# Two rearrangements in the opening of an adaptive-norm transformer block: part of the modulation's second half summed off TensorE, and the second segment's norm placed ahead of the first attention blocks

## The chip, the core and the metric

The kernel is one launch on one core of a Trainium2 chip. The core's engines run side by side, each with its own queue of instructions: TensorE (PE; its weight loads are PEld), VectorE (DVE), ScalarE (ACT), GpSimd (POOL) and SyncE (SP), which here issues nearly all DMAs. The metric is device time in microseconds (us), the median of three runs.

## What is computed

One block of a transformer on 2048 rows of 512 columns, all in float32. A vector `c` gives six rows of 512 by a matrix product (the modulation); two of them, `sa` and `ca`, shift and scale the first norm.

```python
mod = (_silu(c) @ w_mod).reshape(c.shape[0], 6, 1, -1)
sa, ca, ga, sb, cb, gb = (mod[:, i] for i in range(6))
h = _layernorm(x, axis=-1) * (1 + ca) + sa
x = x + ga * _A_ref(h, A_wq, A_wk, A_wv, A_wo, A_beta)      # attention
h = _layernorm(x, axis=-1) * (1 + cb) + sb
x = x + gb * _B_ref(h, B_w_gate, B_w_up, B_w_down)          # (h Wg * h Wu) Wd
# in _A_ref, for each of N = 4 segments of 512 rows, 32 heads of 16:
logits = einsum("bhqd,bhkd->bhqk", qs, ks) * scale + mask   # causal inside the segment
a_dot = einsum("bhqk,bhkd->bhqd", softmax(logits), vs)
a_mem = (phi(qs) @ M) / (phi(qs) . z + 1e-6)                # memory of earlier segments
o = g * a_mem + (1 - g) * a_dot
M = M + phi(ks)^T @ vs;  z = z + sum(phi(ks))               # phi(t) = t + 1 if t > 0 else exp(t)
```

## The kernel before

The rows go in four segments of 512, each as four tiles of 128 rows; the 32 heads go in four groups `g` of eight. A float32 product is made of three products of split numbers (a rounded high part `H` and the rest `L`); scores are made of three bfloat16 parts of keys and queries, which are written to memory (`kd`, `qd`) and read back stacked (`kst`, `qst`).

**The opening** runs alone, before attention starts. SP issues the loads of `c` (into `s_c`), four tiles of `x` (`xload(0)`), and the first half of two columns of blocks of `w_mod` (`wm0_load(0)`), then key, query and value weights among the second half. PE is kept busy by 20 matmuls of zeros (`NWU`, `warm`). `mod0(j)` makes half `j` of `sa` and `ca` on PE: for each block `k` of 128 rows of `w_mod` and each of four blocks of columns a matmul with `s_c[:, k]`, repeated over 96 columns, into bank `mp0[j]` (tile `m`). `ln(...)`, for segment 0 in its `first` form, makes the norm: statistics by `bn_stats` and `bn_aggr`, one over the root of the variance by a logarithm and an exponential on ACT with one Newton step (tiles `sd`, `y`, `a`, `b`, which the profile calls `asd`, `ay`, `aya`, `ayb`), the normalization of the four tiles in place, PE transposes into `atp`, the modulation on ACT (`ahf`), and the split (`ahH`, `ahL`). Then `a_kq(0, g, "k" or "q")` makes keys and queries of a group (`kps`, `qps`, then `kf`, `qf`), cuts them in three, and makes the features `phi` (`phk`, `phq`); `a_v(0)` makes the values (`vps`, `v`). `gates()` makes `gg` and `omg` from `beta`, copies `omg` into the values' tiles on POOL, and scales the head masks `hmg`. `load_g(nm, w, g)` loads and splits a group's weights (`wrk` into `wkH`, `wkL`); the loads land in tiles that `staged` takes from a list of tags.

**The attention loop** (`for v in range(-2, NQ + 1)`, L1151) goes over 32 units of four heads. `q_half` multiplies queries by keys into two alternating banks, and a DVE instruction reduces each result to its row maximum (`nm`); `k_step` makes the scores again with the maximum in them, ACT takes the exponential (`pt`), POOL masks the diagonal, `av_step` multiplies by the values. Between these steps `fill` takes pieces of the next work from the generator `fill_a`: keys and queries of the next groups, the next segment's norm, the memory.

**What sets the order.** PE's instructions are chained in the order in which the code issues them. `CV` and `CA` chain instructions of DVE and ACT in the same way (`Chain`, L39 in the profile); `vec` and `act` leave the order to a scheduler at build time, until `vec.eng = CV` is set at L1149. POOL's order is the scheduler's. In segment 0, `fill_a` loads segment 1's `x` when it comes to group 2, and weaves the first nine steps of that norm (four tiles of statistics, the root, four normalizations) into the matmuls of groups 2 and 3:

```python
if g >= 2 and s + 1 < NSEG:
    if g == 2:
        xts[s + 1] = xload(s + 1)
        lns = a_ln(s + 1)
        Q = weave(Q, lns, (0, 1, 2, 3))
    else:
        K = weave(K, lns, (1,) if s > 0 else (0, 1, 3))
        Q = weave(Q, lns, (0, 1, 2, 3) if s > 0 else (0, 1))
```

For that norm ACT makes `sd` and `y`, and POOL the five small steps. After the loop the second half of the block follows in its own stage, which the change does not touch.

Of the kernel before, what the change touches and what calls it, by code (L numbers as in the profile page):

```python
# [8 lines left out]
F32 = mybir.dt.float32  # L9
F32R = mybir.dt.float32r  # L10
BF = mybir.dt.bfloat16
AF = mybir.ActivationFunctionType
ALU = mybir.AluOpType
# [4 lines left out]
P = 128  # L18
S, D, H, DH, NSEG, L, F = 2048, 512, 32, 16, 4, 512, 1376
KT = D // P  # L20
# [37 lines left out]
def tile_kernel(ctx, tc, x, wq, wk_, wv, wo, beta, w_gate, w_up, w_down, c, w_mod, out):  # L58
    nc = tc.nc
# [24 lines left out]
    def MM(*a, **k):  # L84
        return pe(nc.tensor.matmul(*a, **k))  # L85
# [4 lines left out]
    CV, CA = Chain(tc, nc.vector), Chain(tc, nc.scalar)  # L90
    vec, act = Switch(nc.vector), Switch(nc.scalar)
# [50 lines left out]
    ones = cst.tile([P, P], F32, name="ones")  # L142
# [29 lines left out]
    def ln(pool, hpool, xt, s, sc, sh, pfx, hb, fast):  # L172
# [10 lines left out]
            if not first:  # L183
                yield 0.0
        sd = pool.tile([P, 4], F32, tag="sd", name=f"{pfx}sd{s}", bufs=2)
        A.activation(sd, mv[:, :, 1], AF.Ln, bias=epst[:, 0:1])
        y = pool.tile([P, 4], F32, tag="y", name=f"{pfx}y{s}", bufs=2)
        A.activation(y, sd, AF.Exp, scale=-0.5)
        a = pool.tile([P, 4], F32, tag="ya", name=f"{pfx}ya{s}", bufs=2)
        b = pool.tile([P, 4], F32, tag="yb", name=f"{pfx}yb{s}", bufs=2)  # L190
        eng = CV if first else nc.gpsimd
        eng.tensor_mul(a, y, y)
        if first:
            CV.scalar_tensor_tensor(b, mv[:, :, 1], EPS, a, op0=ALU.add, op1=ALU.mult)
        else:
            eng.tensor_scalar(b, mv[:, :, 1], 1.0, EPS, op0=ALU.mult, op1=ALU.add)
            eng.tensor_mul(b, b, a)
# [44 lines left out]
    def run(gen):  # L242
        try:
            while True:
                next(gen)
        except StopIteration as e:
            return e.value

    apool, ap = open_pool(name="ap", bufs=1)
    PT = 6  # L250
# [374 lines left out]

    pwpool, pw = open_pool(name="pw", bufs=1, reuse_waits="tile")
    papool, pa = open_pool(name="pa", bufs=2, reuse_waits="tile")
    nc.sync.dma_start(s_c, c)
    wm = w_mod.rearrange("(k p) n -> p k n", p=P)

    def load_mod(i):
# [7 lines left out]
    def xload(s):  # L639
        xt = []  # L640
        for t in range(4):
            a = pa.tile([P, D], F32, tag="x", name=f"x{s}_{t}", bufs=4)
            pin(nc.sync.dma_start(a, x[rows(s, t), :]))
            xt.append(a)
        return xt

    xts = {0: xload(0)}
    NWU = 20
    wu = pa.tile([P, 512], BF, tag="rl", name="wu", bufs=1)
    vec.memset(wu, 0.0)  # L650
    wups = psp.tile([P, 2, 512], F32, tag="lk", name="wups", bufs=1)
# [64 lines left out]
        CV.tensor_copy(sa_c[:, 2 * j:2 * j + 2], ps[:, 0:2])  # L716
        CV.tensor_scalar_add(ca_c[:, 2 * j:2 * j + 2], ps[:, 2:4], 1.0)

    def mod0(j):
        ps = mp0[j].rearrange("p (i n) -> p i n", n=P)[:, :, 0:MW]  # L720
        for k in range(KT):
            for i in range(4):
                MM(ps[:, i], r0[j][k][:, i * P:(i + 1) * P], s_c[:, k:k + 1].to_broadcast([P, MW]),
                   start=k == i == 0, stop=k == KT - 1, skip_group_check=True)

    hcur = [None]

    def a_ln(s):
        return ln(pa, pa, xts.pop(s), s, ca_c, sa_c, "a", ("h", 8, 2), s == 0)

    def weave(a, b, at):

        i = 0
        for w in a:
            yield w
            if w:
                for _ in range(at.count(i)):
                    w = next(b, None)
                    if w or w is False:
                        yield w  # L740
                i += 1

    wH, wL = {}, {}
    stage = [("ph", 3), ("ph", 3), ("ph", 3), ("mem", 1), ("pkr", 1), ("f", 2)] + [("x", 4)] * 4 + [("mem", 1), ("memb", 2)]
    nst = [0]

    def staged(nm):
        tg, n = stage[nst[0] % len(stage)]
        nst[0] += 1
        return (ap if tg == "memb" else pa).tile([P, D], F32, tag=tg, name=f"wr{nm}", bufs=n)  # L750

    def load_g(nm, w, g):
# [46 lines left out]
    def a_kq(s, g, nm):  # L799
# [3 lines left out]
        if True:  # L803
# [2 lines left out]
            n = 0  # L806
            three = ((wH, hH), (wH, hL), (wL, hH)) if s == 0 and g < 2 else ((wH, hH), (wL, hH), (wH, hL))
            terms = [(k, *ab) for k in range(KT) for ab in three]
            if s == 0 and g == 1:
                terms.sort(key=lambda t: t[1] is wL)  # L810
            for k, a, b in terms:
                MM(ps, a[nm, g][:, k, :], b[k], start=n == 0, stop=n == 11)
                n += 1
# [2 lines left out]
            f = pa.tile([P, L], F32, tag="f", name=f"{nm}f{s}_{g}", bufs=2)  # L816
            fast = s == 0 and g == 0
            A, V = (CA, CV) if fast else (act, nc.gpsimd)
            A.activation(f, ps, AF.Copy)
            q3 = pa.tile([P, 3, L], BF, tag="q3", name=f"{nm}3_{s}_{g}", bufs=2)  # L820
            r = pa.tile([P, L], F32, tag="qr", name=f"{nm}r_{s}_{g}", bufs=2)
            i0, i1, i2 = (0, 1, 2) if nm == "k" else (2, 1, 0)
# [153 lines left out]
    def fill_a():  # L976
# [1 line left out]
            next(w)  # L978
        yield from av
        memq.extend((a_mem(0, 0), a_mem(0, 1)))  # L980
        lns = None
        for s in range(NSEG):
            if s > 0:
                hcur[0] = yield from lns
# [2 lines left out]
            for g in range(2 if s == 0 else 0, NG):  # L987
# [5 lines left out]
                K, Q = a_kq(s, g, "k"), a_kq(s, g, "q")  # L993
                if s == NSEG - 1 and g == 0:
                    B["orl"] = wo_load(0, wpool)
                if g >= 2 and s + 1 < NSEG:
                    if g == 2:
                        xts[s + 1] = xload(s + 1)
                        lns = a_ln(s + 1)
                        Q = weave(Q, lns, (0, 1, 2, 3))  # L1000
                    else:
                        K = weave(K, lns, (1,) if s > 0 else (0, 1, 3))
                        Q = weave(Q, lns, (0, 1, 2, 3) if s > 0 else (0, 1))
                if g == 1 and 0 < s < 3:
                    acc = mod_acc(r)
                    K, Q = weave(K, acc, (0, 2)), weave(Q, acc, (0, 2))
# [98 lines left out]
    lng = ln(pa, pa, xts.pop(0), 0, ca_c, sa_c, "a", ("h", 8, 2), True)  # L1105
    next(lng)
    mod0(0)
    next(lng)
    mod0_out(0, mp0[0])
    mod0(1)  # L1110
    next(lw[0])
    next(lng)
    next(lng)
# [13 lines left out]
    w1 = [load_g(nm, w, 1) for nm, w in (("k", wk_), ("q", wq))]  # L1127
    for w in w1:
        next(w)
    run(kq0[1])  # L1130
    run(kq0[0])
    load(0)
# [4 lines left out]
        next(w)  # L1137
    for i in range(3):
        next(av)
    gates()  # L1140
    w2 = [load_g(nm, w, 2) for nm, w in (("k", wk_), ("q", wq))]
    for w in w2:
# [536 lines left out]
```

## Time and profile before

| | |
|---|---|
| runs | 854.02, 854.42, 854.63 us; median 854.42 us |
| profiled execution | 853.83 us, of which the span of the trace is 852.1 us |
| busy in the span | PE 98%, DVE 75%, ACT 58%, POOL 32% |
| chain that ended last | PE 60%, DVE 4%, ACT 2%, POOL 2% of the span |
| DMA | 139.57 MB, mean 164 GB/s |
| granted TensorE clock | 1.0 |

Times in the profile count from the span's start. A row of the timeline gives start, duration, engine, line of the kernel, operation, written and read tiles (buffer numbers left out), and in brackets the idle time before it with what ended it. A group's row gives the sum, the mean of one in ns, and the idle time before. A matmul's end is modelled, so two matmuls in a row seem to overlap. Spans on POOL are rough.

### The profile page before, as it was taken

What the parts mean: (1) busy time and instruction counts of PE and PEld (TensorE: products, weight loads), DVE (VectorE), ACT (ScalarE), POOL (GpSimd) and SP (SyncE); (2) the same over time, 40 slices, a digit from 0 to 9 for tenths busy, and PEclk for the clock granted to TensorE, in tenths of its full rate; (3) what the DMA queues carried; (4) which work ended last, traced back from release to release, by engine and by line L of the source; (5) the groups of instructions that cost most, each with busy time, mean ns of one, the idle gap of its engine ahead of it and who ended that gap; (6) DMA issues with size and microseconds to landing.
All of it is one profiled execution on the core that took longest, in us unless ns stands there. A gap on an engine that the chain in (4) does not pass through costs nothing.

```text
span 852.1 us, 14420 instructions
## 1 busy us (share of the span) xinstructions
PE 835.4 (98%) x4982; PEld 598.2 (70%) x4982; DVE 641.9 (75%) x1796; ACT 498.0 (58%) x759; POOL 275.7 (32%) x423
## 2 busy tenths in 40 slices
PE   9989999999999999999999999999999999999998
PEld 6756656666665656656665687887888778888886
DVE  7897868887778967787888359989987855447654
ACT  4758767787676876677545626344435546455230
POOL 2756627566565774675424610000000000000000
PEclk9999999999999999999999999999999999999999
DMA  9655445564545554457675457587650675335102
GB/s 272 153 150 158 111 114 136 164 171 120 144 103 166 146 163 106 123 155 230 173 233 161 137 193 238 187 286 273 233 220 28 234 269 211 123 135 185 42 9 98
DMA packets 83928, 139.57 MB, mean 164 GB/s; under 512 B 12720, under 2 KB 46768, under 8 KB 83856
## 3 DMA queue, kind: packets, MB, share of 16 engines
q1 hardware_dynamic: 83568, 138.52, 52.6%
q8 instruction: 39, 0.64, 0.3%
q14 instruction: 33, 0.27, 0.1%
q10 hardware_dynamic: 288, 0.15, 0.1%
HBM read 89.87 MB, written 48.50 MB: 162 GB/s over the span
## 4 chain that ended last, share of the span: by engine, by line
PE 60%; DVE 4%; ACT 2%; POOL 2%; issue 1%; DMA 0%; DVEq 0%; POOLq 0%; ACTq 0%
PE acc L1355 14%; PE Xu L1286 7%; PE Xg L1286 7%; PE wops L85 5%; PE tb L85 4%; PE Yu L1286 4%; PE Yg L1286 4%; PE k L85 3%; PE q L85 3%; DVE q L39 2%; PE Zg L1286 1%; PE Zu L1286 1%; PE qps L85 1%; PE vps L85 1%; PE ctp L88 1%; PE Xx L1286 1%
## 5 line engine op out<-in xcount | busy, mean ns | idle before, releaser
L39 DVE CUSTOM_DVE_ANT_0 q<-q,cmask 128x384 f32<-128x384 f32 (+3 forms) x512 | 248.3, 503 | 72.2 <-PE q L85 64.6
L335 ACT ACTIVATE pt<-k 128x1024 f32<-128x1024 f32 x160 | 163.9, 1024 | 74.2 <-PE k L85 72.2
L341 POOL TENSOR_SCALAR_AFFINE_SELECT pt<-pt 128x256 f32<-128x256 f32 (+1 forms) x224 | 97.6, 449 | 137.9 <-ACT pt L335 135.9
L85 PE MATMUL q<-kst,qst 96*128 96x384 bf16 (+3 forms) x512 | 122.8, 302 | 6.4 <-DVE nm L39 5.1
L85 PE MATMUL k<-qst,kst 98*128 98x384 bf16 (+3 forms) x512 | 96.0, 299 | 1.6 <-ACT pt L335 1.3
L1363 DVE TENSOR_TENSOR xa<-xa,acc 128x512 f32<-128x512 f32 x95 | 64.9, 684 | 39.1 <-PE acc L1355 38.5
L85 PEld LDWEIGHTS <-qst 96*128 96x128 bf16 x512 | 43.9, 98 | 57.8 <-issue 43.0
L85 PE MATMUL tb<-pt,v 128*32 128x512 f32 (+3 forms) x1024 | 75.7, 436 | 0.3 <-POOL pt L341 0.3
L39 DVE DVE_READ_ACCUMULATOR2_ANT nm<- 128x1 f32 x512 | 72.0, 141 | 0.0
L85 PEld LDWEIGHTS <-kst 98*128 98x128 bf16 x512 | 44.5, 98 | 25.0 <-issue 8.8
L1355 PE MATMUL acc<-dH,mH 128*128 128x512 f32 (+1 forms) x152 | 60.3, 397 | 0.0
L1355 PE MATMUL acc<-dL,mH 128*128 128x512 f32 (+1 forms) x152 | 60.1, 395 | 0.0
L1355 PE MATMUL acc<-dH,mL 128*128 128x512 f32 (+1 forms) x152 | 60.0, 395 | 0.0
L85 PEld LDWEIGHTS tb<-pt,v 128*32 128x32 f32 x1024 | 28.6, 109 | 39.2 <-issue 35.5
L367 ACT ACTIVATE tsb<-tb 128x512 f32<-128x512 f32 x32 | 19.1, 596 | 31.7 <-PE tb L85 31.6
L1355 PEld LDWEIGHTS acc<-dL,mH 128*128 128x128 f32 (+1 forms) x152 | 28.6, 188 | 7.1
L1355 PEld LDWEIGHTS acc<-dH,mL 128*128 128x128 f32 (+1 forms) x152 | 28.5, 188 | 7.1 <-DVE mL L1306 0.3
L1355 PEld LDWEIGHTS acc<-dH,mH 128*128 128x128 f32 (+1 forms) x152 | 28.5, 188 | 6.7
L85 PE MATMUL kps<-ahH,wkH 128*128 128x512 f32 x64 | 29.5, 460 | 0.0
L85 PE MATMUL qps<-ahH,wqH 128*128 128x512 f32 x64 | 28.7, 449 | 0.0
L85 PE MATMUL wops<-woH,oH 128*128 128x512 f32 x64 | 28.3, 442 | 0.0
L85 PE MATMUL vps<-wvH,ahH 128*128 128x512 f32 x64 | 28.3, 442 | 0.0
(399 smaller groups left out, 2018.4 us busy)
## 6 DMA issues: line engine op xcount, KB each, us to landing
wm<-in_w_mod_dram SPq DMA_DIRECT2D x24, 256.0 KB, 4.6
kd<-k SPq DMA_DIRECT2D x16, 384.0 KB, 2.5
qd<-q SPq DMA_DIRECT2D x16, 384.0 KB, 3.3
kst<-kd SPq DMA_DIRECT2D x32, 192.0 KB, 3.3
qst<-qd SPq DMA_DIRECT2D x32, 192.0 KB, 3.8
x<-in_x_dram SPq DMA_DIRECT2D x16, 256.0 KB, 4.7
kst<-kd SPq DMA_DIRECT2D x32, 128.0 KB, 3.2
qst<-qd SPq DMA_DIRECT2D x32, 128.0 KB, 3.8
```

Of the source, the lines that this page charges most:

```text
L39: i = getattr(self.eng, name)(*a, **k)
L85: return pe(nc.tensor.matmul(*a, **k))
L88: return pe(nc.tensor.transpose(*a))
L335: ex = act.activation(pt, kp, AF.Exp, scale=0.25)
L341: sels[u, i] = nc.gpsimd.affine_select(w, w, pattern=[[0, w.shape[1]], [1, P]], compare_op=ALU.is_ge, fill=0.0, base=0, channel_multiplier=-1)
L367: act.activation(tsbs[u], tbs.pop(u), AF.Copy)
L1286: pe(nc.tensor.matmul(ps[0:n], a, b[:, k], start=first and c == 0, stop=last and c == 5, skip_group_check=True))
L1355: pe(nc.tensor.matmul(ps, a[0:m, t * P:(t + 1) * P], b[0:m], start=j == 0, stop=j == n - 1))
L1363: vec.tensor_add(xa, xa, ps)
```

## The change

In the opening's modulation, the second half (`mod0(1)`) leaves out block 0 on PE: ACT scales block 0 by `s_c[:, 0]` in place, DVE multiplies block 1 by `s_c[:, 1]` and adds block 0 to it, and PE multiplies the sum by ones; blocks 2 and 3 stay as they were. `c` is loaded from ACT's queue and not from SP's, and there are 18 warm-up matmuls, not 20.

Segment 1's norm leaves the loop. Its `x` is loaded right after the weights of group 1, and its first nine steps are issued ahead of `gates()`, with DVE's steps chained by `CV`, ACT's two by `CA`, and the five small steps on DVE (in four instructions) and not on POOL. The later steps (transposes, modulation, split) stay at the start of segment 1. So that `x` can be loaded early, four of the weights' staging tiles come from the tag `pt` and not from `x`. In segment 0 the terms of groups 0 and 1 are put in another order on PE (products with the weights' low part later), and ACT's first copies of group 1's keys and queries are chained.

```diff
         sd = pool.tile([P, 4], F32, tag="sd", name=f"{pfx}sd{s}", bufs=2)
-        A.activation(sd, mv[:, :, 1], AF.Ln, bias=epst[:, 0:1])
+        E = CA if s < 2 else act
+        E.activation(sd, mv[:, :, 1], AF.Ln, bias=epst[:, 0:1])
         y = pool.tile([P, 4], F32, tag="y", name=f"{pfx}y{s}", bufs=2)
-        A.activation(y, sd, AF.Exp, scale=-0.5)
+        E.activation(y, sd, AF.Exp, scale=-0.5)
...
-        eng = CV if first else nc.gpsimd
+        eng = CV if s < 2 else nc.gpsimd
         eng.tensor_mul(a, y, y)
-        if first:
+        if s < 2:
             CV.scalar_tensor_tensor(b, mv[:, :, 1], EPS, a, op0=ALU.add, op1=ALU.mult)
...
-    nc.sync.dma_start(s_c, c)
+    nc.scalar.dma_start(s_c, c)
...
-    NWU = 20
+    NWU = 18
...
-    def mod0(j):
+    def mod0(j, ks=range(KT)):
         ps = mp0[j].rearrange("p (i n) -> p i n", n=P)[:, :, 0:MW]
-        for k in range(KT):
+        for k in ks:
+            f = s_c[:, k:k + 1].to_broadcast([P, MW]) if len(ks) == KT or k > 1 else ones[:, 0:MW]
             for i in range(4):
-                MM(ps[:, i], r0[j][k][:, i * P:(i + 1) * P], s_c[:, k:k + 1].to_broadcast([P, MW]),
-                   start=k == i == 0, stop=k == KT - 1, skip_group_check=True)
+                MM(ps[:, i], r0[j][k][:, i * P:(i + 1) * P], f,
+                   start=k == ks[0] and i == 0, stop=k == KT - 1, skip_group_check=True)
...
-    stage = [("ph", 3), ("ph", 3), ("ph", 3), ("mem", 1), ("pkr", 1), ("f", 2)] + [("x", 4)] * 4 + [("mem", 1), ("memb", 2)]
+    stage = [("ph", 3), ("ph", 3), ("ph", 3), ("mem", 1), ("pkr", 1), ("f", 2)] + [("pt", PT)] * 4 + [("mem", 1), ("memb", 2)]
...
-            if s == 0 and g == 1:
-                terms.sort(key=lambda t: t[1] is wL)
+            if s == 0 and g < 2:
+                terms.sort(key=lambda t: (t[0] // 2 if g == 0 else 0, t[1] is wL))
...
-            A.activation(f, ps, AF.Copy)
+            (CA if s == 0 and g < 2 else act).activation(f, ps, AF.Copy)
...
-        lns = None
+        lns = ln1
...
-                if g >= 2 and s + 1 < NSEG:
+                if g >= 2 and 0 < s < NSEG - 1:
...
-                        K = weave(K, lns, (1,) if s > 0 else (0, 1, 3))
-                        Q = weave(Q, lns, (0, 1, 2, 3) if s > 0 else (0, 1))
+                        K = weave(K, lns, (1,))
+                        Q = weave(Q, lns, (0, 1, 2, 3))
...
     mod0(0)
+    CA.activation(r0[1][0], r0[1][0], AF.Copy, scale=s_c[:, 0:1])
     next(lng)
     mod0_out(0, mp0[0])
-    mod0(1)
+    CV.scalar_tensor_tensor(r0[1][1], r0[1][1], s_c[:, 1:2], r0[1][0], op0=ALU.mult, op1=ALU.add)
+    mod0(1, (1, 2, 3))
...
     for w in w1:
         next(w)
+    xts[1] = xload(1)
     run(kq0[1])
...
     for i in range(3):
         next(av)
+    vec.eng = CV
+    ln1 = a_ln(1)
+    for _ in range(9):
+        next(ln1)
     gates()
```

More of the change, by code (lines that the diff above doesn't have):

```diff
@@ L749, in staged @@
         nst[0] += 1
+        if tg == "pt":
+            return ap.tile([P, 2, 512], F32, tag=tg, name=f"wr{nm}", bufs=n)[:, 0]
         return (ap if tg == "memb" else pa).tile([P, D], F32, tag=tg, name=f"wr{nm}", bufs=n)
```

## The prediction

> **What bounds the kernel now.** I read the page first, then the busy time by stretches, then what TensorE waited for, and last the timeline of the first 80 us, engine by engine. The page, part 1, gives busy time and share of the span for each engine:
>
> ```profile
> PE 835.4 (98%) x4982; PEld 598.2 (70%) x4982; DVE 641.9 (75%) x1796; ACT 498.0 (58%) x759; POOL 275.7 (32%) x423
> ```
>
> TensorE (PE) is the bound, so what counts is where it stands still. The busy time in three stretches (start:end, width, then busy us and instruction count of PE, PEld, DVE, ACT, POOL, then the granted clock) and what PE waited for between 50 and 80 us:
>
> ```profile
> 34.00:50.00 16.00, 14.71 (x77) 10.18 (x75) 14.72 (x45) 7.34 (x11) 11.66 (x12) 1.00 0.75 189
> 50.00:80.00 30.00, 27.46 (x185) 18.03 (x184) 27.69 (x102) 22.20 (x35) 16.89 (x27) 1.00 0.45 121
> 80.00:128.00 48.00, 48.00 (x351) 29.84 (x348) 33.98 (x129) 34.97 (x48) 23.75 (x37) 1.00 0.48 130
> ```
>
> ```profile
> PE q L85 <- DVE nm L39: 1.8, 5, 0.7
> PE k L85 <- ACT pt L335: 0.7, 2, 0.6
> ```
>
> From 80 us on PE never stops. Between 50 and 80 us it is idle for 30 - 27.46 = 2.5 us, and most of that is the score matmuls `q` waiting until VectorE (DVE) has read the bank before (`nm`): segment 0's attention is held by DVE, which is busy 27.69 of 30 us there.
>
> **The opening's modulation.** The timeline of the first 26 us (start, duration, engine, line, operation, out<-in), and the median landing time of one load, the second block of the second half, issued at 6.65:
>
> ```profile
> 0.82 0.38 SPq L628 DMA_DIRECT2D s_c<-in_c_dram  x1
> ...
> 1.26 1.85 SPq L643 DMA_DIRECT2D x<-in_x_dram  x4
> ...
> 2.09 0.15 PEld L85 LDWEIGHTS <-wu 128*128 128x128 bf16 x1 [0.27 <-issue]
> ...
> 5.50 0.15 PEld L85 LDWEIGHTS <-wu 128*128 128x128 bf16 x1 [0.27 <-issue]
> ...
> 5.89 1.82 PEld L85 LDWEIGHTS <-wu 128*128 128x128 bf16 x9 [0.24 <-issue]
> ...
> 8.21 3.78 PE L85 MATMUL m<-s_c,wm 128*128 128x96 f32 x32
> ...
> 13.57 3.71 PE L85 MATMUL m<-s_c,wm 128*128 128x96 f32 x32
> ...
> 15.21 0.51 SPq L758 DMA_DIRECT2D wrq<-in_wq_dram  x1
> ...
> 25.48 0.37 SPq L829 DMA_DIRECT2D kd<-k  x1
> ```
>
> ```profile
> wm<-in_w_mod_dram SPq DMA_DIRECT2D x1, 256.0 KB, 6.1
> ```
>
> ```order
> L88 MATMUL atp_3_322<-ident,x_3_208 128x128
> L85 MATMUL m_251<-s_c,wm_0_233 128x96 x4
> L85 MATMUL m_251<-s_c,wm_1_234 128x96 x4
> L85 MATMUL m_251<-s_c,wm_2_235 128x96 x4
> L85 MATMUL m_251<-s_c,wm_3_236 128x96 x4
> L85 MATMUL kps_0_379<-ahH_0_365,wkH_253 128x512
> ```
>
> That was PE before, from the last transpose to the first keys; this is PE after the change:
>
> ```order
> L88 MATMUL atp_3_321<-ident,x_3_208 128x128
> L85 MATMUL m_249<-ones,wm_1_232 128x96 x4
> L85 MATMUL m_249<-s_c,wm_2_233 128x96 x4
> L85 MATMUL m_249<-s_c,wm_3_234 128x96 x4
> L85 MATMUL kps_0_375<-ahH_0_361,wkH_251 128x512
> ```
>
> One of four blocks is gone, 3.71 / 4 = 0.93 us of PE. The load of `c` leaves SP's queue, so `x` and the weights behind it are issued 1.26 - 0.82 = 0.44 us earlier; two warm-up matmuls fewer free PE 2 x 1.82 / 9 = 0.40 us earlier. Together 1.3 us (`kps` at 15.7 and not 17.0). Its cover: the second block lands at 6.65 + 6.1 - 0.44 = 12.3, DVE's sum (0.69, by the fused row below) ends at 13.0, and PE wants it at 13.57 - 0.40 = 13.17. If that cover goes, each tenth is lost again; bounds 0.9 and 1.4. The wait that ScalarE's scaling adds stands ahead of `wkH`; PE needs that only after the second half, so I cost it at nothing. The four loads of segment 1's `x` now go into SP's queue behind 15.21; SP has nothing else until 25.48, so they cost nothing there and land ten microseconds before their use.
>
> **The norm's new place.** Here the 1.3 us may be lost again. DVE before, from the last cut of the first queries to the first score reduction (`phk` features, `omg`/`gg` gates, `ISA q` the reduction):
>
> ```order
> L39 TENSOR_TENSOR q_0_0_444<-qr_0_445,q_0_0_444 128x512
> L39 SCALAR_TENSOR_TENSOR phk_0_451<-phk_0_451,rlk_0_452 128x512
> L39 TENSOR_SCALAR omg<-omg 128x32
> L39 TENSOR_SCALAR gg<-gg 128x32
> L39 RECIPROCAL gg<-gg 128x32
> L39 RECIPROCAL omg<-omg 128x32
> L852 SCALAR_TENSOR_TENSOR phk_1_543<-phk_1_543,rlk_1_544 128x512
> L39 ISA q_0_0_594,nm_593<-q_0_0_594,cmask 128x512
> ```
>
> And after:
>
> ```order
> L39 SCALAR_TENSOR_TENSOR phk_0_455<-phk_0_455,rlk_0_456 128x512
> L39 BN_STATS ast_0_499<-x_0_435 128x6
> ...
> L39 BN_AGGR amv_498<-ast_3_508 128x2
> L39 TENSOR_TENSOR aya_515<-ay_513 128x4
> L39 SCALAR_TENSOR_TENSOR ayb_516<-amv_498,aya_515 128x4
> L39 TENSOR_SCALAR ayb_516<-ayb_516 128x4
> L39 TENSOR_TENSOR ay_513<-ay_513,ayb_516 128x4
> L39 TENSOR_SCALAR x_0_435<-x_0_435,amv_498,ay_513 128x512
> ...
> L39 TENSOR_SCALAR omg<-omg 128x32
> ...
> L39 SCALAR_TENSOR_TENSOR phk_1_574<-phk_1_574,rlk_1_575 128x512
> L39 ISA q_0_0_625,nm_624<-q_0_0_625,cmask 128x512
> ```
>
> Sixteen instructions now stand between the features of groups 0 and 1, all ahead of the first reduction. On GpSimd (POOL), whose work in these microseconds is splits of weights (`wkL`, `wqL`) and keys (`kr`, `k`), and the copies of the gate (`v`), after:
>
> ```order
> L768 TENSOR_TENSOR wqL_433<-wrq_431,wqH_432 128x4x8x16
> L768 TENSOR_TENSOR wkL_549<-wrk_547,wkH_548 128x4x8x16
> L768 TENSOR_TENSOR wqL_553<-wrq_551,wqH_552 128x4x8x16
> L828 TENSOR_TENSOR kr_1_571<-kf_1_568,k_0_1_570 128x512
> L684 COPY v_0_162<-omg 128x32
> ...
> L832 TENSOR_TENSOR k_0_1_570<-kr_1_571,k_0_1_570 128x512
> ```
>
> Before, the copies came ahead of group 2's splits; now both splits and `kr` are ahead of them, beside the norm. What that does is read from DVE before:
>
> ```profile
> 27.12 2.19 DVE L39 SCALAR_TENSOR_TENSOR phk<-phk,rlk 128x512 f32<-128x512 f32 x1
> 29.23 1.65 DVE L39 TENSOR_SCALAR omg<-omg 128x32 f32<-128x32 f32 x1
> ...
> 32.27 0.35 DVE L39 RECIPROCAL omg<-omg 128x32 f32<-128x32 f32 x1 [0.91 <-POOL v L683]
> 33.71 3.76 DVE L852 SCALAR_TENSOR_TENSOR phk<-phk,rlk 128x512 f32<-128x512 f32 x1 [1.08 <-ACT phk L847]
> 37.39 0.69 DVE L39 CUSTOM_DVE_ANT_0 q<-q,cmask 128x512 f32<-128x512 f32 x1
> ...
> 53.48 0.69 DVE L39 SCALAR_TENSOR_TENSOR phk<-phk,rlk 128x512 f32<-128x512 f32 x1
> ```
>
> and from POOL, ScalarE (ACT) and PE at the same time:
>
> ```profile
> 26.96 1.81 POOL L764 TENSOR_TENSOR wkL<-wrk,wkH 128x512 fp32r<-128x512 f32 x1 [18.46 <-ACT wkH L39]
> 28.72 2.13 POOL L764 TENSOR_TENSOR wqL<-wrq,wqH 128x512 fp32r<-128x512 f32 x1
> 30.95 1.29 POOL L683 COPY v<-omg 128x32 f32<-128x32 f32 x8
> ...
> 33.61 1.70 POOL L764 TENSOR_TENSOR wkL<-wrk,wkH 128x512 fp32r<-128x512 f32 x1
> 35.17 1.69 POOL L764 TENSOR_TENSOR wqL<-wrq,wqH 128x512 fp32r<-128x512 f32 x1
> ...
> 37.81 1.33 POOL L824 TENSOR_TENSOR kr<-kf,k 128x512 f32<-128x512 f32 x1
> ```
>
> ```profile
> 31.38 0.60 ACT L819 ACTIVATE kf<-kps 128x512 f32<-128x512 f32 x1
> 32.01 0.63 ACT L823 ACTIVATE k<-kf 128x512 bf16<-128x512 f32 x1
> ```
>
> ```profile
> 36.49 0.40 PE L85 MATMUL vps<-wvH,ahL 128*128 128x512 f32 x1
> 36.73 0.40 PE L85 MATMUL vps<-wvL,ahH 128*128 128x512 f32 x1
> ...
> 37.66 0.39 PE L85 MATMUL q<-kst,qst 96*128 96x512 bf16 x1
> ```
>
> The same fused instruction takes 0.69 us at 53.48, 2.19 at 27.12 and 3.76 at 33.71; the long ones end just after a POOL instruction with two inputs ends (28.77, 36.86). The two engines shut each other out. [...]
>
> The norm's own durations are in segment 0's first norm; the rows after are the groups of DVE work between 50 and 76 us that the change takes away there:
>
> ```profile
> 5.22 0.69 DVE L39 BATCH_NORM_STATS2 ast<-x 128x6 f32<-128x512 f32 x1 [0.48 <-DMA x<-in_x_dram]
> ...
> 8.34 0.18 DVE L39 BATCH_NORM_AGGREGATE amv<-ast 128x2 f32<-128x6 f32 x1
> ...
> 9.12 0.16 DVE L39 TENSOR_TENSOR aya<-ay 128x4 f32<-128x4 f32 x1 [0.60 <-ACT ay L39]
> ...
> 9.92 1.92 DVE L39 TENSOR_SCALAR x<-x,amv,ay 128x512 f32<-128x512 f32 x4
> ```
>
> ```profile
> L39 DVE BATCH_NORM_STATS2 ast<-x 128x6 f32<-128x512 f32 x4 | 2.7, 682 | 0.0
> L39 DVE TENSOR_SCALAR x<-x,amv,ay 128x512 f32<-128x512 f32 x4 | 2.3, 578 | 0.4 <-POOL ay L199 0.4
> ```
>
> Step by step, each time 1.3 us earlier than before. The features of group 0 end at 27.12 + 2.19 - 1.3 = 28.0. Statistics take 8.34 + 0.18 - 5.22 = 3.3: 31.3. ACT's logarithm and exponential take 9.12 - 8.52 = 0.6: 31.9. POOL is then in group 2's splits: 28.72 + 2.13 - 1.3 = 29.55, plus two (35.17 + 1.69 - 33.61 = 3.25), ends 32.8, so the next DVE step waits 0.9 us. Four small steps take 9.92 - 9.12 = 0.8: 33.6. Meanwhile ACT, held by the norm until 31.9, does `gg`, `kf` and `k` (0.1 + 0.6 + 0.6): `kr` is ready at 33.2 and shuts DVE out for one piece, about 1.2 of its 1.33: 34.8. Four normalizations, 1.92: 36.7. Then `omg` (0.2), the eight copies on POOL that it releases (1.29, with 0.1 on each side) and the reciprocal (0.35): 38.7. By then POOL is in `k`, again 1.2 us after the copies' end at 38.3: 39.4. The fused step, 0.69: the first reduction starts at about 40.0, against 37.39. Without any exclusion it would be 40.0 - 0.9 - 1.2 - 0.7 = 37.2; if a fused step loses one more round, as at 33.71, 41.2. I take 39.9, nearest to what rows show beside POOL: **2.5 us later**. PE's third score matmul needs the first bank back, so all of PE's order shifts by it; the 1.3 us of the opening are inside this number. Behind the waiting ACT stand `kf` and all that follows, at 32.0 and not at 31.38 - 1.3 = 30.1; who waits for that is `kr`, which is counted.
>
> What comes back: 2.7 + 2.3 = 5.0 us of DVE work are gone between 50 and 76 us. PE's five recorded waits for DVE there are 1.8 us. A matmul shows 0.40 and the next starts 36.73 - 36.49 = 0.24 later, so every wait hides 0.16 more: 0.8 for five. Of ACT's 0.7 I count 0.3. **2.9 us earlier**; ends 1.8 (recorded waits alone) and 4.1 (the 2.5 us of idle and twice the hidden part). POOL loses the norm's small steps there, which I cost at nothing: it is busy 16.89 of the 30 us.
>
> Sum: +2.5 - 2.9 = -0.4 us. The profiled execution took 853.83 us (span 852.1 and 1.7 around it), so 853.4 by its own time; the median of the runs shown is 0.6 above it, so 854.0 as a median. A difference under 0.2% (1.7 us) is about what a measurement of this kernel cannot tell from none.
>
> **Rivals.** *Exclusions fall open.* If POOL waits as often as DVE does, the first reduction starts near 37.2 (0.2 before today's) and DVE's relief is whole with ACT's part: -0.2 - 3.0 = -3.2, 851.2. For it: at 27.12 the fused step got in between two splits, and `wqL` took 2.13 there, not 1.69. Against it: 33.71.
>
> *PE goes cold.* PE reaches its third score matmul at 37.66 + 0.2 - 1.3 = 36.6 and gets it 0.8 after the first reduction starts: 4.1 us idle with 39.9, where its longest wait in the rows above is 0.7. The warm-up rows show what cold costs: nine weight loads from 2.09 to 5.50 are 0.43 apart, later nine 0.20, though the granted clock reads 1.00 in the stretches; the slow part lasts from 1.7 to 5.9, 4.2 us at half speed, 2.1 us lost. If one fused step also loses a round, +1.3. It decides from a first reduction past about 40.5: +2.5 + 1.3 - 2.9 + 2.1 = +3.0, 857.4. [...]
>
> *The relief is not PE's.* Only the 1.8 us recorded come back, other engines hold the rest: +0.7, 855.1. ACT's 22.2 of 30 us speak against it.
>
> **Numbers.** The forecast 0.41 (faster 0.08, within 0.2% 0.32, slower 0.01), the first rival 0.29 (faster 0.28, same 0.01), cold PE 0.20 (same 0.03, slower 0.17), relief lost 0.10 (same 0.06, slower 0.04). Faster 0.36, within 0.2% 0.42, slower 0.22. The range goes from 851.2, the first rival, to 857.0, most of the second; the forecast's own is 852.5 to 855.2.
>
> **What would show it.** Right: `kps` near 15.7; `kr` ahead of the copies; the first reduction at 39.5 to 40.5 with PE idle about 4 us before it; no waits of `q` for DVE between 52 and 80. Wrong: a first reduction before 38.5 (first rival), score matmuls twice as far apart after the gap (second), `q` still waiting after 55 (third), or a second modulation half that starts late because its sum does.

## The result: 857.71 us against 854.42, 0.4% slower

| | before | after |
|---|---|---|
| median of 5 runs | 854.42 us (853.90 to 854.84) | 857.71 us (856.55 to 858.14) |
| ratio, 95% interval | | 1.0037 [1.0025, 1.0048] |
| profiled execution | 853.83 us, span 852.1 | 858.14 us, span 856.4 |

The forecast was 854.0 in a range of 851.2 to 857.0. What came is, within 0.3 us, the rival called "PE goes cold" (857.4), whose own sum lay above the range that was given. The page of the changed kernel, part 1, shows the same totals as before:

```profile
PE 836.3 (98%) x4972; PEld 598.3 (70%) x4972; DVE 642.6 (75%) x1801; ACT 498.0 (58%) x760; POOL 275.0 (32%) x418
```

So the 4.3 us between the two profiled executions (the medians are 3.3 apart; the profiled one is the slowest of the changed kernel's five) are time in which PE stands still or runs slowly. The same stretches as before (PE, PEld, DVE, ACT, POOL, then the granted clock), and behind them three stretches of 3.41 us around the place where the clock changes:

```profile
34.00:50.00 16.00, 12.08 (x45) 7.82 (x44) 11.16 (x33) 6.01 (x13) 8.39 (x21) 0.79 0.46 116
50.00:80.00 30.00, 28.37 (x194) 19.18 (x194) 25.50 (x102) 20.91 (x31) 14.61 (x19) 1.00 0.36 95
...
37.08:40.49 3.41, 1.20 (x4) 0.60 (x5) 2.46 (x8) 1.90 (x4) 2.06 (x10) 1.00 0.01 1
40.49:43.90 3.41, 1.74 (x5) 1.31 (x5) 3.25 (x9) 0.00 (x0) 3.41 (x7) 0.50 0.58 161
43.90:47.32 3.42, 3.42 (x10) 2.28 (x9) 1.38 (x5) 0.62 (x1) 1.81 (x6) 0.50 0.54 168
```

From 34 to 50 us PE is busy 12.08 us, with 45 matmuls; before it was 14.71, with 77. The clock is 0.5 from 40.49 to 47.32 us, where before it was 1.00. From 50 to 80 us PE is busy 0.9 us more than before (28.37 against 27.46).

Where that comes from stands in the timelines of the changed kernel. PE, around the gap:

```profile
38.32 0.39 PE L85 MATMUL q<-kst,qst 96*128 96x512 bf16 x1
42.16 0.58 PE L85 MATMUL q<-kst,qst 96*128 96x384 bf16 x2 [3.45 <-DVE nm L39]
...
43.08 0.63 PE L85 MATMUL vps<-wvH,ahL 128*128 128x512 f32 x1
43.50 0.63 PE L85 MATMUL vps<-wvL,ahH 128*128 128x512 f32 x1
```

PE waits 3.45 us for the first reduction, and the matmuls behind the gap start 0.42 us apart, where such matmuls started 0.24 apart before (36.49 and 36.73 in the prediction's rows). DVE, from the features of group 0 to that reduction:

```profile
27.04 3.85 DVE L39 SCALAR_TENSOR_TENSOR phk<-phk,rlk 128x512 f32<-128x512 f32 x1
...
34.70 0.16 DVE L39 TENSOR_TENSOR aya<-ay 128x4 f32<-128x4 f32 x1 [0.60 <-ACT ay L39]
...
35.49 2.88 DVE L39 TENSOR_SCALAR x<-x,amv,ay 128x512 f32<-128x512 f32 x4
38.29 0.17 DVE L39 TENSOR_SCALAR omg<-omg 128x32 f32<-128x32 f32 x1
...
39.85 0.35 DVE L39 RECIPROCAL omg<-omg 128x32 f32<-128x32 f32 x1 [0.92 <-POOL v L684]
40.12 1.32 DVE L39 SCALAR_TENSOR_TENSOR phk<-phk,rlk 128x512 f32<-128x512 f32 x1
41.36 0.68 DVE L39 CUSTOM_DVE_ANT_0 q<-q,cmask 128x512 f32<-128x512 f32 x1
```

and POOL beside it:

```profile
26.87 1.85 POOL L768 TENSOR_TENSOR wkL<-wrk,wkH 128x512 fp32r<-128x512 f32 x1 [18.66 <-ACT wkH L39]
28.63 1.71 POOL L768 TENSOR_TENSOR wqL<-wrq,wqH 128x512 fp32r<-128x512 f32 x1
30.30 2.14 POOL L768 TENSOR_TENSOR wkL<-wrk,wkH 128x512 fp32r<-128x512 f32 x1
...
36.01 1.17 POOL L828 TENSOR_TENSOR kr<-kf,k 128x512 f32<-128x512 f32 x1 [1.98 <-ACT k L827]
```

The features of group 0 (27.04) came 0.17 us after a split had begun, and ended at 30.89, just after the second split ended (30.34). The normalizations took 2.88 and not 1.92 us, with `kr` between them. The first reduction starts at 41.36 and not at 37.39.

And the opening, PE first, then DVE's wait for `x`:

```profile
8.81 3.78 PE L85 MATMUL m<-s_c,wm 128*128 128x96 f32 x32 [0.77 <-DVE ast L39]
14.28 1.13 PE L85 MATMUL m<-ones,wm 128*128 128x96 f32 x8
...
16.98 0.47 PE L85 MATMUL kps<-ahH,wkH 128*128 128x512 f32 x1
```

```profile
6.08 0.69 DVE L39 BATCH_NORM_STATS2 ast<-x 128x6 f32<-128x512 f32 x1 [0.80 <-DMA x<-in_x_dram]
```

The first half of the modulation starts 0.60 us later than before (8.81 against 8.21), although PE has two warm-up matmuls fewer, since the statistics it follows wait for `x`. What the second half saves is used up by that: the keys come at 16.98, before 17.07.

The start of the same matmuls in the two traces, after minus before (medians over the stretch, in the time of before):

| 16 to 36 us | 36 to 40 | 40 to 52 | 56 | 64 | to the end |
|---|---|---|---|---|---|
| -0.09 | +3.97 | +6.29 | +4.82 | +4.18 | +4.32 |

The late reduction gives +4.1 (from -0.09 to +3.97), half clock +2.3 (to +6.29), the relief -2.1 (to +4.18), and little happens after 64 us. For the same three sizes in the experiments, this table gathers them; "shift" is that of PE's order against before ahead of 36 us, from 40 to 50 us, and behind 64 us. From about 365 us on single traces move by up to 0.7 us either way, which no experiment here follows up. The last four columns are from the one profiled execution of each kernel:

| kernel | median us | ratio to before, 95% interval | keys start | first reduction | half clock, us | shift |
|---|---|---|---|---|---|---|
| after | 857.71 | 1.0037 [1.0025, 1.0048] | 16.98 | 41.36 | 6.83 | -0.1, +6.3, +4.2 |
| warm_gap | 854.15 | 0.9992 [0.9982, 1.0001] | 17.11 | 40.62 | none | 0.0, +3.2, +1.1 |
| norm_only | 857.16 | 1.0029 [1.0019, 1.0039] | 17.27 | 40.78 | 3.41 | +0.2, +4.9, +2.7 |
| mod_only | 853.50 | 0.9985 [0.9976, 0.9995] | 16.78 | 37.09 | none | -0.3, -0.3, -0.3 |
| be_late | 855.88 | 1.0018 [1.0008, 1.0027] | 15.90 | 39.53 | 3.41 | -1.1, +3.6, +1.7 |
| mod_late | 852.61 | 0.9979 [0.9969, 0.9988] | 15.63 | 35.96 | none | -1.4, -1.4, -1.4 |
| before_late | 854.16 | 0.9997 [0.9988, 1.0006] | 16.89 | 37.12 | none | -0.2, -0.3, -0.3 |
| psum | 853.97 | 0.9996 [0.9986, 1.0005] | 16.84 | 39.04 | 3.41 | -0.2, +3.2, +1.1 |
| gates_early | 852.10 | 0.9973 [0.9962, 0.9984] | 15.29 | 37.26 | 3.41 | -1.8, +1.4, -0.9 |
| gates_warm | 853.38 | 0.9989 [0.9980, 0.9998] | 15.23 | 36.77 | none | -1.8, +0.3, -2.0 |
| best_w2 | 849.62 | 0.9943 [0.9928, 0.9958] | 15.40 | 34.74 | none | -1.7, -2.0, -4.2 |
| best_again | 849.60 | 0.9947 [0.9934, 0.9961] | 15.44 | 34.80 | none | -1.6, -1.9, -4.2 |

### The profile page after: what moved, and what is told of

The parts are those of the page before. It is cut to its first block, busy times and chain, and to the rows that moved or that the text cites. A ratio compares the mean times of both kernels' runs of the same rounds, so it can differ in the third digit from the quotient of the medians.

```text
span 856.4 us, 14414 instructions
## 1 busy us (share of the span) xinstructions
PE 836.3 (98%) x4972; PEld 598.3 (70%) x4972; DVE 642.6 (75%) x1801; ACT 498.0 (58%) x760; POOL 275.0 (32%) x418
## 4 chain that ended last, share of the span: by engine, by line
PE 58%; DVE 4%; ACT 2%; POOL 2%; DMA 1%; issue 1%; SPq 0%; DVEq 0%; POOLq 0%; ACTq 0%
PE acc L1366 14%; PE Xu L1297 6%; PE Xg L1297 6%; PE wops L85 5%; PE tb L85 4%; PE Yu L1297 4%; PE Yg L1297 4%; PE k L85 3%; PE q L85 3%; DVE q L39 2%; PE Zg L1297 1%; PE Zu L1297 1%; PE qps L85 1%; PE vps L85 1%; DMA crd<-in_w_down_dram 1%
```

## Experiments

### The clock: matmuls in the gap (warm_gap)

The changed kernel, with 28 matmuls of ones into a bank that nothing reads any more, ahead of the third score matmul. They add work and take none away.

```diff
+            if v == -2 and slot == 3:
+                ob = ones.bitcast(BF)
+                for _ in range(28):
+                    MM(wups[:, 0, 0:256], ob[:, 0:P], ob, start=True, stop=True)
             if 0 <= u < NQ:
                 q_half(u, i, 0)
```

> Theory (PE goes cold): in the changed kernel PE stands still for 3.45 us before its third score matmul, and the trace then grants half the clock for 6.8 us. Twenty-eight matmuls of constants (256 columns) in that gap should keep the clock at 1.0 through the loop, and the order behind the gap should win about 2.3 us: 855.4 us. Rival (the gap alone costs, the clock only falls where PE waits for VectorE anyway): no gain, 857.7, or up to 0.5 us more because the matmuls stand in PE's order.

PE around the gap, and the stretches, of this kernel:

```profile
37.88 3.22 PE L85 MATMUL wups<-ones 128*128 128x256 bf16 x28
41.41 0.38 PE L85 MATMUL q<-kst,qst 96*128 96x384 bf16 x2 [0.31 <-DVE nm L39]
```

```profile
34.00:50.00 16.00, 14.71 (x87) 10.76 (x86) 13.61 (x44) 6.77 (x12) 8.84 (x22) 1.00 0.42 114
```

The score matmul still comes only after the reduction, at 41.41, but the clock stays at 1.00, and the ratio falls from 1.0037 to 0.9992: matmuls that compute nothing win 3.8 us (each ratio is known to about 1 us). In the trace, PE's order is 3.0 us earlier than in the changed kernel after the gap, of which 0.74 are the reduction's (40.62 against 41.36: the features of group 0 took 2.19 us in this run) and 2.3 the clock's. So half clock is the largest part of the loss; without it the change cannot be told from the kernel before (the interval of 0.9992 reaches 1.0001). The relief in this trace is 3.25 - 1.1 = 2.1 us.

### The two parts alone (norm_only, mod_only)

The kernel before with the norm's part of the diff and none of the opening's, and the other way round. The second takes these edits, with the order of group 0's and 1's terms:

```diff
-    nc.sync.dma_start(s_c, c)
+    nc.scalar.dma_start(s_c, c)
...
-    NWU = 20
+    NWU = 18
...
-    mod0(1)
+    CV.scalar_tensor_tensor(r0[1][1], r0[1][1], s_c[:, 1:2], r0[1][0], op0=ALU.mult, op1=ALU.add)
+    mod0(1, (1, 2, 3))
```

> The kernel before with the norm's part alone (segment 1's x loaded early, its norm ahead of the gates, the staging tags), modulation as before. Theory: the first score reduction still starts near 41 us, PE stands still over 3 us and falls to half the clock: 857.5 to 858 us. Rival (the loss needs both parts): 854 us.

> The kernel before with the modulation's part alone (block 0 summed off PE, the load of c from ACT's queue, 18 warm-up matmuls, the order of the terms). Theory (the opening's gain is eaten by loads that land later): keys start within 0.2 us of before, 854.3 us. Rival (the opening gains its 0.9 to 1.3 us, and only the norm loses): 853.1 to 853.5 us.

The norm alone costs 0.29% (2.5 us) and the modulation alone gains 0.15% (1.3 us by the times, interval 0.4 to 2.1; its trace shows 0.3 up to 64 us and 0.5 at the end; its keys start 0.29 earlier, so that the times are nearer to the rival and the trace to the theory). The norm's trace has the gap and half clock as well:

```profile
27.33 2.19 DVE L39 SCALAR_TENSOR_TENSOR phk<-phk,rlk 128x512 f32<-128x512 f32 x1
```

Here the features fit in between two splits (2.19 us), and only 3.41 us are at half clock, which cost 1.5 us (shift +3.4 ahead, +4.9 behind). The two parts do not add up to the whole (2.5 - 1.3 = 1.2 us against 3.2 by the ratio): in the trace of after the reduction costs 0.9 us more than in norm_only, and half clock 0.8 more, since it lasts twice as long.

### What held the opening: the load of `beta` (be_late, mod_late, before_late)

`beta` is loaded once for each of 128 partitions, 128 bytes each, on ScalarE's queue at the program's start. Three kernels load it on SP's queue behind the values' weights: the changed one, the one before with the modulation's part, and the one before.

```diff
-    nc.scalar.dma_start(be, beta[None, :].to_broadcast([P, H]))
...
     next(lw[2])
+    nc.sync.dma_start(be, beta[None, :].to_broadcast([P, H]))
...
-        act.activation(omg, be, AF.Exp)
+        CA.activation(omg, be, AF.Exp)
```

> The changed kernel with the load of beta (128 packets of 128 bytes) put behind the values' weights on SP's queue, and its exponential moved with it to the gates. Theory (these small packets, beside the x loads, are what slows x between 3 and 5.5 us): the four x tiles land 1.5 to 2.5 us earlier, the keys start near 15.3 instead of 17.0, and the whole order with them: 856.0 us. Rival (x is slow for another reason): keys at 17.0, 857.7 us.

> The kernel before with the modulation's part and the late load of beta, no norm moved. Theory (beta's packets cost the opening 1.1 us): keys start 0.8 to 1.1 us before those of mod_only, 852.4 us. Rival: VectorE's lock with GpSimd eats it, 853.5 as mod_only.

> The kernel before, with one edit: the gate's vector beta is loaded on SyncE's queue behind the values' weights (and its exponential chained on ScalarE). Theory (beta's 128 small packets slow the loads of x): before's x lost little to them, since x flowed only after them; but they held the DMA engines until 4.0 us, so x should land earlier and the first half of the modulation start 0.3 to 0.6 us before 8.21; the second half waits for PE alone, so the keys come by the same, at 16.5 to 16.8 and not 17.07; time -0.3 to -0.6, ratio 0.9993 to 0.9997. Rival (it was the move of c to ScalarE's queue that held the loads): no change, 8.2 and 17.05.

The row of GB/s in the view of the DMA, in steps of 0.2 us over the first 8 us; of the changed kernel, of before, and of the one with the modulation's part and the late load:

```profile
GB/s 0 0 0 0 0 0 0 0 0 102 92 164 329 351 311 238 230 120 83 36 104 145 75 88 77 93 50 77 219 291 390 389 420 399 379 379 384 379 389 379
```

```profile
GB/s 0 0 0 0 0 0 0 0 0 10 16 21 67 60 19 51 38 37 60 63 297 390 389 348 369 359 369 410 389 400 358 394 389 359 374 389 374 384 384 369
```

```profile
GB/s 0 0 0 0 0 0 0 0 0 82 82 82 257 308 340 363 421 389 379 318 379 389 246 215 374 348 333 297 358 384 384 379 389 374 353 374 353 328 356 358
```

Before, the small packets run from 2 to 4 us, and `x` flows after them at 297 to 410 GB/s. In the changed kernel `x` starts first, and the rate falls to 36 to 145 GB/s from 3.6 to 5.6 us: `x` and `beta` are in flight together then (119 packets under 512 bytes beside 75 larger ones). With `beta` late the dip is gone. The first half of the modulation then starts when PE has done its warm-up:

```profile
7.74 3.71 PE L85 MATMUL m<-s_c,wm 128*128 128x96 f32 x32
13.04 1.03 PE L85 MATMUL m<-ones,wm 128*128 128x96 f32 x8
...
15.63 0.48 PE L85 MATMUL kps<-ahH,wkH 128*128 128x512 f32 x1
```

The keys come at 15.63, 1.4 us before 17.07, and PE's order is 1.4 us earlier at the end too; the ratio is 0.9979 [0.9969, 0.9988]. In the kernel before, the late load alone is worth 0.2 to 0.3 us in the trace and nothing in the times (0.9997), since 20 warm-up matmuls keep PE until 8.1 us in any case. So neither edit alone brings the forecast gain: `c` off SP's queue and fewer warm-up matmuls let the work start earlier, and `beta` out of the way lets `x` be there. In the changed kernel the late load brings the keys to 15.90 and the ratio to 1.0018; half clock and the long gap stay.

That the keys start at 15.90 in be_late, at 15.63 in mod_late and at 15.29 in gates_early (below) is not explained by the edits. PE's warm-up is the same in all three, 18 matmuls from 1.7 us on, and its weight loads are 0.43 us apart at first and about 0.20 later. The change of pace comes at 6.72, 6.23 and 5.03 us (be_late, mod_late, gates_early):

```profile
6.72 0.96 PEld L85 LDWEIGHTS <-wu 128*128 128x128 bf16 x5 [0.21 <-issue]
```

```profile
6.23 1.18 PEld L85 LDWEIGHTS <-wu 128*128 128x128 bf16 x6 [0.15 <-issue]
```

```profile
5.03 1.82 PEld L85 LDWEIGHTS <-wu 128*128 128x128 bf16 x9 [0.23 <-issue]
```

The first half of the modulation follows at 8.01, 7.74 and 7.19 us, about half the difference each time. So the opening of a single trace is known to some tenths of a microsecond only.

`beta` on ACT's queue slowed `x` on SP's: a load of `x` took 5.2 us from issue to landing in after and 5.1 in mod_only (medians of four), against 3.7 in be_late and 3.2 in mod_late.

### The exclusion: one operand of the features in PSUM (psum)

DVE's fused step that makes the features reads two tiles in SBUF. Here ACT writes one of them, `rl`, for groups 0 and 1 into the PSUM tile of the warm-up (`wups`), which is free at that time.

```diff
-                rl = pa.tile([P, L], F32, tag="rl", name=f"rl{nm}{s}_{g}", bufs=1)
+                rl = wups[:, g] if s == 0 and g < 2 else pa.tile([P, L], F32, tag="rl", name=f"rl{nm}{s}_{g}", bufs=1)
```

> The changed kernel with one edit: ScalarE writes the relu parts of groups 0 and 1 to PSUM, so VectorE's two fused feature steps read one SBUF input and not two. Theory (two SBUF inputs are what lets GpSimd shut the step out): both fused steps take 0.7 us and not 2.2 to 3.9 and 1.3, the first score reduction comes at 38 to 39.5 instead of 40.6 to 41.4, PE's gap falls under 2.5 us, the clock stays at 1.0, 853 to 854 us. Rival (any VectorE work waits for GpSimd there): the steps keep their length, 857.

```profile
26.88 0.68 DVE L39 SCALAR_TENSOR_TENSOR phk<-phk,wups 128x512 f32<-128x512 f32 x1
...
31.38 0.49 DVE L39 TENSOR_TENSOR aya<-ay 128x4 f32<-128x4 f32 x1 [0.61 <-ACT ay L39]
31.90 1.58 DVE L39 SCALAR_TENSOR_TENSOR ayb<-amv,aya 128x4 f32<-128x4 f32 x1
33.51 1.10 DVE L39 TENSOR_SCALAR ayb<-ayb 128x4 f32<-128x4 f32 x1
...
38.50 0.63 DVE L39 SCALAR_TENSOR_TENSOR phk<-phk,wups 128x512 f32<-128x512 f32 x1
```

The same step takes 0.68 and 0.63 us where it took 3.85 and 1.32, beside the same pieces of POOL's work (splits, then `k`): the exclusion was the cause, and one operand out of SBUF ends it for this step. But the norm, now earlier, runs into group 2's splits and `kr`: three of its steps on 128x4 numbers (0.16 to 0.17 each in the changed kernel) take 0.49, 1.58 and 1.10. The last of them reads one tile and a constant, as the normalizations do, which `kr` lengthened to 2.88 us in the changed kernel; so one tile in SBUF does not spare every step. The first reduction, at 39.04, is 2.3 us earlier than in the changed kernel, not by the 3.9 us that the two fused steps saved.

The timed runs of this kernel bear on the price of half clock, without any edit. I had expected the clock to stay whole at a gap of 2 us; its ten timed runs are two groups. Six took 853.4 to 854.0 us, with a mean clock of 0.999 or 1.0 over the span, and four 855.6 to 855.8 with 0.998. The profiled run is one of the latter. The difference of the middles is 1.9 us; 3.41 us at half speed lose 1.7 us, and the shift of PE's order grows by 1.5 across them in this trace (by 1.5 in norm_only, be_late and gates_early too). That half clock is what parts the two groups is argued from these sizes and the mean clock; the gaps of the other nine runs are not on record. The stretches around the fall in the profiled run:

```profile
37.61:41.02 3.41, 1.34 (x7) 0.96 (x6) 2.76 (x9) 0.00 (x0) 3.41 (x10) 1.00 0.23 76
41.02:44.43 3.41, 3.41 (x10) 2.28 (x9) 1.96 (x8) 0.75 (x2) 2.64 (x6) 0.50 0.70 193
```

### The gates' steps out of the way (gates_early), and the clock there (gates_warm)

To `psum` with the late `beta`, the gates' steps on DVE and the copies on POOL are issued ahead of group 0's cuts, where DVE has room; only the reciprocal of `omg` stays behind the norm. gates_warm adds 14 matmuls of ones in its gap, as in the first experiment.

```diff
         CV.tensor_scalar_add(gg, gg, 1.0)
-        for tl in (gg, omg):
-            CV.reciprocal(tl, tl)
+        CV.reciprocal(gg, gg)
...
+    gates()
     for kq in kq0:
         next(kq)
```

> As psum, and the gates (their VectorE steps but one, and GpSimd's copies) moved ahead of group 0's cut, where GpSimd is idle, with beta loaded late on SP's queue. Theory: another 1.5 us earlier on VectorE and 1.1 us from the loads; first reduction near 36 to 37, PE's gap under 1.5 us, 851 to 852 us. Rival (the norm's small steps behind group 2's splits hold everything): first reduction past 38, 853 us or more.

> gates_early, and 14 more matmuls of ones on TensorE in the 1.8 us gap ahead of the third score matmul, so that TensorE is busy there; nothing else. Theory (clock): the half clock of 3.413 us from 39.12 goes away, and with it 1.0 to 1.7 us; the first reduction stays at 37.3, the shift of PE's order from 64 us on goes from -0.87 to about -2.2; time about 850.8, ratio to before 0.996. Rival (the gap alone, and the half clock is hidden behind the softmax engines there): no gain, 852.1. From best_w2, which closes the gap in another way, the difference that is left is then the pure price of the wait, 1 to 1.5 us.

The first reduction comes at 37.26, the ratio is 0.9973. What is left is one step of the norm, shut out by POOL through the rest of one piece and two more (`wkL` until 31.22, `wqL` until 32.85, `kr` until 33.97), then the gap, and 3.41 us at half clock after it:

```profile
30.09 3.90 DVE L39 TENSOR_TENSOR aya<-ay 128x4 f32<-128x4 f32 x1 [0.60 <-ACT ay L39]
```

```profile
38.06 0.38 PE L85 MATMUL q<-kst,qst 96*128 96x384 bf16 x2 [1.79 <-DVE nm L39]
```

```profile
35.71:39.12 3.41, 1.62 (x9) 0.98 (x8) 3.41 (x10) 0.26 (x1) 2.24 (x6) 1.00 0.00 0
39.12:42.53 3.41, 3.41 (x11) 2.24 (x10) 1.99 (x9) 0.62 (x1) 1.83 (x2) 0.50 0.89 239
```

A gap of 1.79 us was enough. In gates_warm the clock stays at 1.00, but the filling does not lie in the gap as in the first experiment: the matmuls of ones write the tile `wups`, which the features now read, and so they wait for DVE:

```profile
36.90 1.69 PE L85 MATMUL wups<-ones 128*128 128x256 bf16 x14 [0.72 <-DVE phk L39]
38.43 0.38 PE L85 MATMUL q<-kst,qst 96*128 96x384 bf16 x2
```

The score matmul behind them starts 1.66 us after the first reduction (36.77); in gates_early it was 0.80. PE's order was still 1.1 us ahead of gates_early from 40 us on, since that trace has the half clock, but at about 370 us 0.6 of it were lost again, and the timed median is 853.38, not earlier than 852.10 but later. Six of the seven timed runs of gates_early had a mean clock of 0.999 or 1.0, so they had little to win, and against them the score matmul's later start is a loss of 0.4 us (38.43 against 38.06). With the 0.6 that is most of the 1.3 us; the rest stays open, and this run is no clean test of the clock.

### The splits out of the way (best_w2, best_again)

One line more: ACT's rounding of group 2's weights is chained behind group 1's first copies, and so POOL's splits come after the norm.

```diff
-        A, V = CA if g < 2 else act, CV if g == 0 else nc.gpsimd
+        A, V = CA if g < 3 else act, CV if g == 0 else nc.gpsimd
```

> As gates_early, with ScalarE's part of group 2's splits held behind group 1's first copies, so that GpSimd splits after the norm. Theory (GpSimd's splits are what holds the norm's small steps): first reduction near 35 to 35.5, no gap on PE, 850.5 us. Rival (the late splits make group 2's keys wait): PE waits for the weights' low part near 40 us, 852 us or more.

> The same kernel as best_w2, timed in more rounds beside the other two. 849.2 to 850.3, ratio to before 0.993 to 0.996; clock 1.0 throughout, first reduction 34.7. If its four runs before were lucky in the clock, some runs come at 851 to 853.

DVE and POOL of this kernel:

```profile
30.23 0.17 DVE L39 TENSOR_TENSOR aya<-ay 128x4 f32<-128x4 f32 x1 [0.61 <-ACT ay L39]
...
31.02 2.77 DVE L39 TENSOR_SCALAR x<-x,amv,ay 128x512 f32<-128x512 f32 x4
...
33.98 0.62 DVE L39 SCALAR_TENSOR_TENSOR phk<-phk,wups 128x512 f32<-128x512 f32 x1
34.74 0.70 DVE L39 CUSTOM_DVE_ANT_0 q<-q,cmask 128x512 f32<-128x512 f32 x1
```

```profile
28.00 1.67 POOL L770 TENSOR_TENSOR wqL<-wrq,wqH 128x512 fp32r<-128x512 f32 x1
31.42 1.18 POOL L830 TENSOR_TENSOR kr<-kf,k 128x512 f32<-128x512 f32 x1 [1.75 <-ACT k L829]
...
34.77 1.63 POOL L770 TENSOR_TENSOR wkL<-wrk,wkH 128x512 fp32r<-128x512 f32 x1
```

The norm meets only `kr` now, the first reduction comes at 34.74, 2.6 us ahead of before, no gap is left, and the clock stays at 1.00. Both times it was measured the kernel took 849.6 us: ratio 0.9943 [0.9928, 0.9958] and 0.9947 [0.9934, 0.9961]. That is 0.5% faster than before and 0.9% faster than the change as it was made. In the trace the idea of the change, the norm off the loop, was good for 2.2 us (from -2.0 to -4.2), and the opening for 1.7 (some tenths of it by the warm-up's pace); in the change as it was made, the norm's placing lost all that and more.

## Why the prediction was wrong, step by step

| step | predicted | measured in after |
|---|---|---|
| keys start | 15.7 | 16.98 |
| features of group 0 | 2.19 long, end 28.0 | 3.85 long, end 30.9 |
| statistics, root | 3.3, 0.6 | 3.28, 0.60 |
| wait for group 2's splits | 0.9 | 0 |
| normalizations with `kr` | 1.92 + 1.2 | 2.88 |
| first reduction | 39.9 | 41.36 |
| score matmul's wait | 4.1 | 3.45 |
| half clock | 0 (2.1 in the rival) | 2.3 |
| relief from 50 to 80 us | 2.9 | 2.1 |

The forecast's sum was +2.5 for the late reduction and -2.9 for the relief, -0.4 us. The trace has +4.1, -2.1, and +2.3 for half clock, which the sum put at nothing. So each term failed, by 1.6, 0.8 and 2.3 us, and the largest is half clock, for which the sum had nothing.

**The opening's gain** is the first step that failed: 1.3 us forecast, 0.1 measured. The 0.44 us for the earlier issue of `x` counted SP's queue alone. I did not ask what `c` and `x` would meet on the DMA engines: `beta`'s packets, whose load took 3.7 us to land in the trace of before, and 5.2 in that of after. The 0.93 us of the left-out block were right: with `beta` late the second half takes 2.6 us from its start to the keys (13.04 to 15.63) against 3.5 (13.57 to 17.07), and the whole gain is 1.4 against my 1.3 (that close by luck, since the pace of the warm-up alone moves it by tenths). In after the features of group 0 start 1.2 us later than forecast (27.04 against 25.8) by this step.

**The first reduction** was 1.5 us later than predicted: 1.2 from the opening, 1.7 because the features lost a second round to POOL, less 0.9 since the splits were then done when the small steps came, and less 0.5 in the smaller steps. The mechanism was the one described, and its order of steps came out row for row. Which round a step loses was not foreseen, and stays open: the features began 0.17 us behind the start of a split in after and lost two rounds (3.85 us); they began 0.16 behind one in before and lost one (2.19), and took 2.19 in norm_only and warm_gap too. I took one lost round as the likeliest and put two at an end, which these four traces bear out; whether the other runs of after lost two as well is not on record.

**The clock** was a rival with 0.20, and it decided. Its price came out (2.1 against 2.3) by luck: it was read off the 4.2 us of the warm-up, and 6.83 us ran at half clock here, with PE busy 5.16 of them. Its threshold was wrong: I let it decide from a first reduction past 40.5, as if the gap alone counted. No run shows that figure: the clock fell with first reductions from 37.26 (gates_early) to 41.36 us (after), and stayed at 1.00 with one at 40.62, where the gap was filled (warm_gap). The falls in after, psum and gates_early each follow a stretch of 3.41 us with PE busy 1.20, 1.34 and 1.62 us in it, under half, at single gaps of 3.45, 2.06 and 1.79 us; norm_only and be_late fell behind 0.79 and 0.46 us. The stretches can be counted from the change of pace in the warm-up on, in steps of 3.413 us: in after the warm-up changes pace at 6.36 us, the clock falls 34.13 us later (40.49), which is ten steps, and stays low for two (6.83); in the other four traces with half clock it lasts one (3.41). The warm-up starts at 1.7 us each time, but changes pace at 5.03 us in gates_early and 6.72 in be_late, and there too the fall comes ten steps later, to within 0.08 us (34.09 and 34.06). Counted so in before and after, no stretch with PE busy 2.35 us or more was followed by a fall (the least busy of these is 53.63 to 57.05 us of before, 2.35). The only one between, 1.74 in after from 40.49 us, lay at half clock and kept it. A stretch idle for a little more than half was enough (1.79 of 3.41 us in gates_early). By these falls (an estimate), the forecast's own 4.1 us of idle PE could hardly have stayed warm: however such stretches fall on it, one holds at least half of it, 2.05 us, and leaves PE busy 1.36 at most. So the forecast, with this price left out, was not consistent with its own gap. The rival's 857.4 is near the median for the wrong parts: 3.8 (2.5 and 1.3), -2.9 and 2.1, against 4.1, -2.1 and 2.3 in the trace.

**The relief** was over-sized: 2.1 in after, 1.9 to 2.3 in the other kernels that have the norm's part, for a forecast of 2.9 with ends of 1.8 and 4.1. PE's waits in warm_gap, whose times are nearest to those of before, for the same work (53.2 to 81.1 us, since its order is 3.2 us later at first and 1.1 at the end):

```profile
PE k L85 <- ACT pt L336: 0.9, 2, 0.6
PE q L85 <- DVE nm L39: 0.5, 2, 0.3
```

The recorded waits for DVE fell from 1.8 to 0.5 and from five to two, so they gave 1.3, and the three that went hide 0.5 by the 0.16 that the forecast put to each; the rest of the 2.1 stands in no row. What did not come is the waits that remain, and ACT's part, counted at 0.3: these waits are 0.9, where they were 0.7. The rival "The relief is not PE's" had too little, the forecast too much. That the first rival's exclusions would fall open was not seen in any run without psum's edit.

## What to carry to other kernels

Before work is put into a stretch in which PE runs alone, ask for the longest time PE will then be idle within 3.4 us, and count the clock as part of the price as soon as this nears half: in these traces it fell behind 1.79 us or more of idle time in 3.41, which cost 1.5 to 2.3 us beside a gap of 1.8 to 3.5. A DVE step with two SBUF operands should not be placed beside GpSimd's two-input work on the path that PE waits for (0.69 us became 1.32 to 3.85 here): put one operand in PSUM (0.68 and 0.63 in psum), or move the other engine's work behind it (here 2.5 us by the medians of gates_early and best_w2, with one line); a step that reads one tile can be shut out too (0.17 us became 1.10 in psum), so look at its row. Matmuls that fill a gap must write a tile that nothing uses, or they wait for its readers and hold up what stands behind them (0.4 us in gates_warm). And when a load is moved to another queue, look at which packets will then be in flight with which: 16 KB of small ones beside the load on the path cost the opening about 1.1 us (16.98 in after, 15.90 in be_late).

## What the runs showed of the hardware

- 128 packets of 128 bytes, in flight with 2 KB packets of `x`, held the rate to 36 to 145 GB/s for 2 us (after, 3.6 to 5.6 us), where it is 215 to 389 without them (mod_late, the same time).
- A DVE step of 0.16 us on 128x4 numbers was shut out for 3.90 us (gates_early), through the rest of one GpSimd instruction and two more. The engine shut out did not get its turn when the instruction under way ended.
- The clock fell to half behind stretches of 3.41 us in which PE was busy 0.46 to 1.62 us, at gaps of 1.79 to 3.45 us.
- One kernel (psum), without an edit, ran in two groups 1.9 us apart, with a mean clock of 0.998 in the later one and 0.999 or 1.0 in the other.
